# Gated mix of 32-head attention and a bilinear FFN on one core: a re-planned static schedule, x transposed on TensorE, one activation table, dead buffers reused as exponential tiles

## The chip, the core and the metric

The kernel runs on one core of a Trainium2 chip. The metric is the device time in microseconds (us) of one execution. The engines are TensorE (PE: matmuls; PEld: its weight loads), VectorE (DVE), ScalarE (ACT), GpSimd (POOL) and SyncE (SP, which here only issues DMAs). They run side by side, each works through its own instructions in order, and they wait for each other by semaphores.

## The reference, cut to what matters

```
x  [2048, 512] bf16, 32 heads of 16, F = 1376
g  = sigmoid((x * gate_w).sum(-1))
q, k, v = x @ wqkv
p  = softmax(q k^T / 4)            # per head, 2048 x 2048
a  = (p v) @ wo
b  = ((x @ w_gate) * (x @ w_up)) @ w_down
out = g * a + (1 - g) * b
```

## The kernel before, in words

**Work.** Queries come in 4 chunks of 512, heads in 4 blocks of 8, and a block's heads in two halves of 4. One chunk, block and half is a group: 32 groups, each of 4 heads x 16 key tiles = 64 score tiles of 128 keys x 512 queries, 2048 in all. A visit (L957) issues 2 to 4 score matmuls at once, one head in each 32-row strip of the array, into as many of the 8 PSUM banks. Each score tile is then turned into exponentials in a 512-column cell of the SBUF buffer `PT`, in one of two ways:

- ACT: one instruction for 1, 2 or 3 tiles (L1023), an exact exponential.
- DVE: an integer approximation (L1087) that writes the bits of a bf16. It needs three further copies with an added offset (L1039 on POOL, L1040 on DVE; `NP` = 4 variants in all), each multiplied with a V of its own scaling, so such a tile costs four PV matmuls instead of one.

PV matmuls (L1354; four heads in the four 32-column strips) accumulate a group into one bank, with a column of ones that gives the softmax denominator. Four matmuls that run side by side in the four strips are called a pack here.

**After each group** (`norm`, L1193 and following): DVE copies the bank to `oraw` (L1300); a DMA gathers the denominators into `den4`; DVE takes the reciprocal (L1222); a DMA writes it to `rscr` in DRAM. After the second half of a block four DMAs move rows of `oraw`, a DMA broadcasts `rscr` into `rb`, and POOL multiplies (L1278) into `OT`. All these DMAs go through SP's queue, between the weight loads.

**Products** (`_Fill`, tile4 at L454): K, Q, V, up, gate, down and output projection products of 4 or 11 packs each are put between scores and PV as "fills"; DVE evicts each.

**The order is a plan made when the program is built.** A loop simulates the engines with one cost per instruction: `a_cad(n)` for ACT, `d_cad`/`d_fast` for DVE, `p_cad` for POOL, a latency to the reader each (`A_LAT`, `D_LAT`, `P_LAT`), `PEC` for a pack, `PSW` for a change between row and column tiling, and for each DMA an issue cost (0.08 us) and a time to landing (2.0 to 2.4 us in `norm`, L1203 to L1268). At each simulated moment a policy per engine picks what is ready: `pe_policy` a visit, an urgent fill (`need` close), a PV pack, then any fill; `dve_policy` evictions, exponentials, copies; `pool_policy` first the OT products, then copies. The result is a fixed list of instructions per engine; on the chip each list runs in order whatever the real times are.

**Start and tail.** x of chunk 0 is loaded in 4 DMAs by SP, transposed by 16 TensorE matmuls of 128 columns (L487) and evicted by DVE (L506); chunks 1 to 3 are loaded by 12 transposing DMAs. All of w_down is loaded once into `wd`. The last group has its denominators in a bank of their own (L1365), and in the tail ACT takes Ln (L1557) and Exp (L1558) on four column slices; per slice DVE multiplies (L1561), PE multiplies with `wol` (L1566), DVE combines (L1575) and SP writes the output.

`PT` has `NC` = 34 cells; `xT`, `wk`, `wq`, `wv`, `wug`, `wd`, `hT` are buffers of their own.

Of the kernel before, what the change touches and what calls it, by code (L numbers as in the profile page):

```python
# [143 lines left out]
class _Fill:  # L144

    __slots__ = ("name", "packs", "deps", "evac", "need", "pos", "bank", "ok")

    def __init__(self, name, packs, deps, evac, need=10**9, ok=None):
# [25 lines left out]
def _build(nc, A_x, A_wqkv, A_wo, W_gate, W_up, W_down, gate_w, out):  # L174
# [22 lines left out]
    NC = 34  # L197
    NW = 4
# [7 lines left out]
    SLK = -0.1  # L206
# [4 lines left out]
    A_LAT = 0.24  # L211

    def d_cad(n):
        return 0.09 + n / 960.0

    def d_fast(n):
        return 0.09 + n / 3840.0

    D_LAT = 0.1

    def p_cad(n):
        return 0.2 + n / 1200.0
# [7 lines left out]
    with ExitStack() as stack:  # L230
# [4 lines left out]
        xT = sb("xT", [128, KD, S], BF16)  # L235
        wk = sb("wk", [128, KD, D], BF16)
        wq = sb("wq", [128, KD, D], BF16)
        wv = sb("wv", [128, KD, D], BF16)
        wo = sb("wo", [128, NB, D], BF16)
        wol = sb("wol", [128, D], BF16)  # L240
        wug = sb("wug", [128, NW, 2, KD, 128], BF16)
        wd = sb("wd", [128, FT, D], BF16)
# [4 lines left out]
        PT = sb("PT", [128, NC, 512], I16)  # L247
        OT = sb("OT", [128, 6, 512], BF16)
        hT = sb("hT", [128, FT, 512], BF16)
# [8 lines left out]
        idt = sb("idt", [128, 128], BF16)  # L258
        gex = sb("gex", [128, T], F32)
# [3 lines left out]
        warm = sb("warm", [128, 1], F32)  # L263
# [3 lines left out]
        free = {"pe": 0.3, "act": 0.3, "dve": 0.3, "pool": 0.3, "sp": 0.3}  # L267
# [75 lines left out]
        def dma(rank, dst, src, deps, stream, dur, after=None, eng="sp", **kw):  # L343
            def go(t):
                def fn(e):
                    return e.dma_start(dst, src, **kw)  # L346

                o = issue(eng, t, 0.08, dur, fn, deps(), stream, 16)
                if after is not None:
                    after(o)  # L350
                return o

            sq.append(_Job(rank, 0.08, deps, go))

        def now_dma(eng, dst, src, stream, dur, deps=(), **kw):
            t = max(free[eng], vis(deps))
            return issue(eng, t, 0.08, dur, lambda e: e.dma_start(dst, src, **kw), list(deps), stream, 16)
# [4 lines left out]
        xn = PT[:, 0:4, :].bitcast(BF16)  # L362
        wcol = lambda lo, hi: A_wqkv[:, lo:hi].rearrange("(kt p) n -> p kt n", p=128)
        d_xn = []
        for tt in range(4):
            d_xn.append(now_dma("sp", xn[:, tt, :], x2[tt * 128 : (tt + 1) * 128, :], f"dxn{tt}", 2.2))
        d_wk, d_wq = [None] * NB, [None] * NB
        d_wq[0] = now_dma("act", wq[:, :, 0:128], wcol(0, 128), "dwq0", 2.4)
        d_wk[0] = now_dma("act", wk[:, :, 0:128], wcol(D, D + 128), "dwk0", 2.6)
        d_wv = now_dma("act", wv[:, :, :], wcol(2 * D, 3 * D), "dwv", 4.0)  # L370
        d_xt = [None] * NCH
        for ch in range(1, NCH):
            for kt in range(KD):
                d_xt[ch] = now_dma(
                    "sp",
                    xT[:, kt, ch * 512 : (ch + 1) * 512],
                    x2[ch * 512 : (ch + 1) * 512, kt * 128 : (kt + 1) * 128],
                    f"dx{ch}",
                    2.0,
                    transpose=True,  # L380
                )
            d_xt[ch].vis = 6.0 + 5.0 * ch
            at(d_xt[ch].vis)
        free["sp"] = 4.0
        r_ = now_dma("act", wk[:, :, 128:D], wcol(D + 128, 2 * D), "dwk1", 6.0)
        d_wk[1:] = [r_] * (NB - 1)
        r_ = now_dma("act", wq[:, :, 128:D], wcol(128, D), "dwq1", 7.0)
        d_wq[1:] = [r_] * (NB - 1)
        d_gw = now_dma("act", gw[:, :], gate_w.rearrange("(kt p) -> p kt", p=128), "dgw", 7.0, allow_slow_non_contiguous=True)

        o_wz = now("dve", 0.1, 0.1, lambda v: v.memset(warm[:], 0.0))
        o_act = now("act", 1.4, 0.2, lambda a: a.activation(warm[:], warm[:], ACT.Exp), [o_wz])
        o_iz = now("dve", 0.1, 0.1, lambda v: v.memset(idt[:], 0.0))
# [5 lines left out]
                idt[:], idt[:], pattern=[[-1, 128]], compare_op=ALU.not_equal, fill=1.0, base=0, channel_multiplier=1  # L399
            ),  # L400
            [o_iz],
        )
        m0 = now("dve", 0.1, 0.1, lambda v: v.memset(mask[:], 0.0))
# [27 lines left out]
        def v_cols(k, t):  # L431
# [3 lines left out]
        ev_x = [None] * KD  # L435
        xdep = lambda ch: [ev_x[kt] for kt in range(KD)] if ch == 0 else [d_xt[ch]]
# [6 lines left out]
            "pvq": 0,  # L443
            "port": None,
# [39 lines left out]
        def mk_x(kt):  # L484
            def pk(tt):
                def f(pe, bank):
                    return pe.matmul(  # L487
                        ps[:, bank, tt * 128 : (tt + 1) * 128],
                        xn[:, tt, kt * 128 : (kt + 1) * 128],
                        idt[:],  # L490
                        start=True,
                        stop=True,
                        skip_group_check=True,
                    )

                return f

            def evac(bank, last):
                def after(o):
                    ev_x[kt] = o  # L500
                    release(banks[bank], [o])
                    if kt == KD - 1:
                        for c_ in range(4):
                            release(cells[c_], [o])

                dve_job(0, d_cad(512), lambda: [last], lambda v: v.tensor_copy(xT[:, kt, 0:512], ps[:, bank, :]), after)  # L506

            return _Fill("x", [pk(tt) for tt in range(4)], lambda: d_xn + [o_id], evac, 0)

        def mk_k(b, ch):  # L510
            def evac(bank, last):
                def after(o):
# [17 lines left out]
                    lambda kt: xT[:, kt, ch * 512 : (ch + 1) * 512],  # L530
# [3 lines left out]
                128 * b + 16 * ch,  # L534
            )

        def mk_q(b, c):
            s = (NB * c + b) % NQB

            def evac(bank, last):  # L540
                def after(o):
# [35 lines left out]
                    lambda kt: xT[:, kt, c * 512 : (c + 1) * 512],  # L577
# [4 lines left out]
                lambda: n < 0 or (n, 1) in q_last,  # L582
            )

        def mk_v(t):
            def evac(bank, last):
# [20 lines left out]
                prod(KD, 128, lambda kt, a, e: xT[:, kt, t * 128 + a : t * 128 + e], lambda kt: wv[:, kt, :]),  # L607
                lambda: [d_wv] + xdep(t // 4),
                evac,
                10**7,  # L610
# [4 lines left out]
        def mk_gate():  # L615
            def pk(q):
                def f(pe, bank):
                    r = None
                    for i in range(8 * q, 8 * q + 8):
# [3 lines left out]
                            xT[:, kt, t * 128 : (t + 1) * 128],  # L623
# [34 lines left out]
            return _Fill("gate", [pk(q) for q in range(8)], lambda: [d_gw] + xdep(0) + d_xt[1:], evac, 200)  # L658
# [4 lines left out]
        def load_w(c, f):  # L663
            n = c * FT + f
            w = FW[f]
            for i, src in enumerate((W_up, W_gate)):

                def after(o, i=i):
# [3 lines left out]
                    5 + n,  # L672
                    wug[:, n % NW, i, :, 0:w],
                    src[:, f * 128 : f * 128 + w].rearrange("(kt p) n -> p kt n", p=128),
                    lambda i=i: [w_free.get((n - NW, i))] if n >= NW else [],
                    f"dwug{n % NW}_{i}",
                    2.6,
                    after,
                )
                sq[-1].alt = (lambda i=i: n < NW or (n - NW, i) in w_free)  # L680

        def mk_ug(c, f, i):
# [18 lines left out]
            def evac_g(bank, last):  # L701
                w_free[n, 1] = last

                def after(o):
# [16 lines left out]
                    lambda kt, a, e: wug[:, n % NW, i, kt, a:e],  # L721
                    lambda kt: xT[:, kt, c * 512 : (c + 1) * 512],
# [6 lines left out]
                and (i == 0 or (n in ocopy and (c == 0 or (c - 1, 3) in d_end))),  # L729
            )  # L730
# [3 lines left out]
        def mk_d(c, tt):  # L734
# [14 lines left out]
            def evac(bank, last):  # L749
# [17 lines left out]
                lambda: [d_wd["d"]] + [ev_h[c, f] for f in range(FT)],  # L767
                evac,
                10**9,
                lambda: "d" in d_wd and all((c, f) in ev_h for f in range(FT)) and "g" in ogate and (c == 0 or (c - 1, tt) in bfree),  # L770
# [58 lines left out]
        fills += [mk_x(kt) for kt in range(KD)] + [mk_q(0, 0), mk_k(0, 0)]  # L829
        fills += [mk_v(t) for t in range(4)] + [mk_k(0, 1)] + [mk_v(t) for t in range(4, 8)] + [mk_k(0, 2)]  # L830
        fills += [mk_v(t) for t in range(8, 12)] + [mk_k(0, 3)] + [mk_v(t) for t in range(12, 16)]
# [12 lines left out]
        for c in range(NCH):  # L844
            for f in range(FT):
                load_w(c, f)
        dma(
# [8 lines left out]
        for j in range(4):  # L856
# [9 lines left out]
        dma(  # L866
            3,
            wd[:, 0 : FT - 1, :],
            W_down[0 : (FT - 1) * 128, :].rearrange("(f p) n -> p f n", p=128),
            lambda: [d_xt[NCH - 1]],  # L870
            "dwd",
            8.0,
        )
        dma(
            3,
            wd[0 : FW[-1], FT - 1, :],
            W_down[(FT - 1) * 128 : F, :],
            lambda: [d_xt[NCH - 1]],
            "dwd",
            8.0,  # L880
            lambda o: d_wd.__setitem__("d", o),
        )

# [21 lines left out]
        def visit(t, n, fb):  # L905
# [4 lines left out]
            if n >= 3 and load < DTH and ndve() < 3:  # L910
                nd = 1
                if n == 4 and load < 0.4 and acts > 0.6:
# [4 lines left out]
            for _ in range(nd):  # L917
                cand = [u for u in us if u not in ds]
                ok = []
                for u in cand:  # L920
# [6 lines left out]
                    if m == 0 and kt < 6:  # L927
# [220 lines left out]
        def dve_policy(t):  # L1148
# [16 lines left out]
            if best is not None and best.rank <= 1:  # L1165
                dq.remove(best)
                best.go(t)
                return True
            if dve_pass(t):
# [23 lines left out]
        def norm(m):  # L1193
# [8 lines left out]
            def after(o):  # L1202
                release(banks[bank], [o])  # L1203
                o_tail["o", m] = o
                row0 = 16 - p
# [6 lines left out]
                    2.0,  # L1212
                    dened,
                )
# [11 lines left out]
            def reced(o2):  # L1226
# [6 lines left out]
                    2.0,  # L1233
                    scred,
                )
# [381 lines left out]
```

## Time and profile before

| what | value |
| --- | --- |
| time, median of 3 runs (all) | 816.77 us (817.53, 809.5, 816.77) |
| the profiled execution | 821.65 us |
| its span, first to last instruction | 818.7 us |
| mean granted TensorE clock | 0.937 |
| busy PE / ACT / DVE / POOL | 741.0 / 734.4 / 634.1 / 472.1 us |
| L1023, exponentials on ACT | 720.0 us in 795 instructions |
| first exponential starts, last one ends | 16.75 us, 801.95 us |

A busy PE is not one at its peak, since the ends of pipelined matmuls are modelled: PE counts as busy for nine tenths of the span, though a pack follows the next in about 0.22 us when nothing holds it. In a line of waits the columns are who waited for whom, us in total, how often, and the longest. In a line of windows they are the window, its length, and busy us (instructions) of PE, PEld, DVE, ACT and POOL, then the granted TensorE clock (1.00 or 0.50 at any moment), the DMA share and GB/s.

### The profile page before, as it was taken

How to read it: one execution, taken by the hardware profiler on the slowest of the kernel's cores; microseconds unless marked ns; L12 is line 12 of the kernel's file. 1: busy time of each engine (PE TensorE's matmuls, PEld its weight loads, DVE VectorE, ACT ScalarE, POOL GpSimd, SP SyncE). 2: the span in 40 equal slices, each digit the busy share in tenths (PEclk: the TensorE clock that was granted, in tenths of full speed). 3: DMA queues.
4: the chain of work that ended last, by engine and by line, in shares of the span. 5: the costliest groups of instructions: out<-in, count | busy, mean ns of one | idle time of the engine just before them, and what ended most of it. 6: DMA issues, size and time to landing. Idle time of an engine off the chain costs nothing.

```text
span 818.7 us, 22335 instructions
## 1 busy us (share of the span) xinstructions
PE 741.0 (91%) x8917; PEld 214.3 (26%) x8917; DVE 634.1 (77%) x1232; ACT 734.4 (90%) x814; POOL 472.1 (58%) x538
## 2 busy tenths in 40 slices
PE   5999998998999989898989989899999998998993
PEld 2232322222322222222222222223222222222220
DVE  4798787786787888787885868858898887869682
ACT  2889897997999999899997979979999998989797
POOL 2456666535566665476654665625676676546460
PEclk9999997897999999999997979979999998999597
DMA  8600011121001111110021111100211100000000
GB/s 173 158 3 4 20 22 40 28 51 34 16 22 34 42 21 51 34 35 21 10 54 28 27 44 35 40 3 8 53 29 34 38 22 2 19 6 2 21 9 26
DMA packets 73478, 27.01 MB, mean 33 GB/s; under 512 B 64384, under 2 KB 70432, under 8 KB 73376
## 3 DMA queue, kind: packets, MB, share of 16 engines
q1 hardware_dynamic: 70208, 24.02, 12.9%
q10 hardware_dynamic: 3168, 1.57, 0.8%
q8 instruction: 71, 1.16, 0.6%
q14 instruction: 31, 0.25, 0.1%
HBM read 19.43 MB, written 2.35 MB: 27 GB/s over the span
## 4 chain that ended last, share of the span: by engine, by line
PE 38%; ACT 32%; DVE 8%; issue 7%; DMA 6%; POOL 4%; SPq 4%; ACTq 0%; DVEq 0%; POOLq 0%
ACT PT L1023 31%; PE ps L1354 13%; PE ps L454 13%; PE ps L957 12%; DMA rb<-rscr 5%; DVE PT L1087 5%; SPq L346 3%; POOL PT L1039 3%; DVE PT L1040 2%; POOL OT L1278 1%; DMA PT<-in_A_x_dram 1%; ACT L1558 1%; ACT L1557 1%; PE ps L1365 1%; DVE VV L603 0%
## 5 line engine op out<-in xcount | busy, mean ns | idle before, releaser
L1023 ACT ACTIVATE PT<-ps 128x1024 bf16<-128x1024 f32 (+2 forms) x795 | 720.0, 1029 | 74.3 <-PE ps L957 38.1
L1039 POOL TENSOR_SCALAR PT<-PT 128x1024 int16<-128x1024 int16 (+1 forms) x478 | 428.8, 918 | 242.6 <-DVE PT L1040 178.7
L1087 DVE TENSOR_SCALAR PT<-ps 128x512 int16<-128x512 f32 (+1 forms) x490 | 339.7, 708 | 97.3 <-PE ps L957 73.0
L1354 PE MATMUL ps<-PT,VV 128*32 128x512 bf16 x3581 | 317.2, 404 | 24.3 <-POOL PT L1039 13.4
L957 PE MATMUL ps<-QT,KT 32*128 32x512 bf16 (+1 forms) x2048 | 278.2, 399 | 28.4 <-ACT PT L1023 20.2
L1040 DVE TENSOR_SCALAR PT<-PT 128x512 int16<-128x512 int16 (+1 forms) x455 | 167.2, 421 | 2.2 <-PE ps L1354 0.5
L957 PEld LDWEIGHTS ps<-QT,KT 32*128 32x128 bf16 (+1 forms) x2048 | 70.5, 91 | 308.9 <-ACT PT L1023 98.0
L1354 PEld LDWEIGHTS ps<-PT,VV 128*32 128x32 bf16 x3581 | 81.8, 97 | 168.5 <-issue 83.8
L454 PE MATMUL ps<-xT,wug 128*32 128x512 bf16 x1376 | 123.1, 414 | 1.7 <-DVE PT L1087 0.9
L454 PE MATMUL ps<-wd,hT 128*32 128x512 bf16 (+1 forms) x704 | 53.2, 397 | 0.2 <-DVE PT L1087 0.2
L1278 POOL TENSOR_TENSOR OT<-oraw,rb 128x512 bf16<-128x512 f32 x16 | 20.5, 1281 | 45.9 <-DMA rb<-rscr 42.4
L697 DVE CAST usb<-ps 128x512 bf16<-128x512 f32 (+1 forms) x44 | 30.1, 684 | 18.0 <-PE ps L454 17.7
L454 PEld LDWEIGHTS ps<-xT,wug 128*32 128x32 bf16 x1376 | 30.5, 98 | 46.4 <-issue 32.6
L712 DVE TENSOR_TENSOR hT<-ps,usb 128x512 bf16<-128x512 f32 (+1 forms) x44 | 30.0, 682 | 8.3 <-PE ps L454 8.0
L454 PE MATMUL ps<-xT,wq 128*32 128x512 bf16 x256 | 21.1, 401 | 1.3 <-DVE xT L506 1.2
L1300 DVE COPY oraw<-ps 128x512 f32<-128x512 f32 x31 | 21.1, 680 | 0.2 <-PE ps L1354 0.2
L760 DVE TENSOR_SCALAR bsb<-ps,omg 128x512 bf16<-128x512 f32 x16 | 12.0, 748 | 11.7 <-PE ps L454 11.5
L593 POOL TENSOR_SCALAR VV<-VV 128x528 bf16<-128x528 bf16 x15 | 9.5, 633 | 19.7 <-DVE VV L593 15.2
L454 PE MATMUL ps<-wo,OT 128*32 128x512 bf16 x240 | 20.4, 407 | 0.0
L454 PE MATMUL ps<-xT,wk 128*32 128x512 bf16 x256 | 20.3, 397 | 0.0
L454 PEld LDWEIGHTS ps<-wd,hT 128*32 128x32 bf16 (+1 forms) x704 | 14.6, 97 | 21.6 <-issue 13.7
L546 POOL TENSOR_SCALAR QT<-QT,mask 128x512 bf16<-128x512 bf16 x16 | 11.1, 696 | 15.5 <-DVE QT L566 15.4
(51 smaller groups left out, 154.3 us busy)
## 6 DMA issues: line engine op xcount, KB each, us to landing
wug<-in_B_w_up_dram SPq DMA_DIRECT2D x40, 128.0 KB, 2.2
wug<-in_B_w_gate_dram SPq DMA_DIRECT2D x40, 128.0 KB, 2.2
rb<-rscr SPq DMA_DIRECT2D x15, 256.0 KB
out_dram<-ost SPq DMA_DIRECT2D x16, 128.0 KB, 1.7
oraw<-oraw SPq DMA_DIRECT2D x60, 32.0 KB, 2.0
wd<-in_B_w_down_dram SPq DMA_DIRECT2D x1, 1280.0 KB, 6.5
PT<-in_A_x_dram SPq DMA_DIRECT2D x4, 128.0 KB, 4.0
wv<-in_A_wqkv_dram ACTq DMA_DIRECT2D x1, 512.0 KB, 7.6
```

The source lines that it names most:

```text
L346: return e.dma_start(dst, src, **kw)
L454: r = pe.matmul(ps[32 * i : min(w, 32 * i + 32), bank, :], lhs(32 * i, min(w, 32 * i + 32)), rhs, start=s0, stop=s1, tile_position=(0, 32 ...
L697: lambda v: v.tensor_copy(usb[0:w, n % 2, :], ps[0:w, bank, :]),
L712: lambda v: v.tensor_tensor(hT[0:w, f, :], ps[0:w, bank, :], usb[0:w, n % 2, :], ALU.mult),
L957: r = pe.matmul(ps[:, bank_of[u], :], KT[32 * j : e, b, kt * 128 : (kt + 1) * 128], QT[32 * j : e, s, p, :], start=True, stop=True, tile_p ...
L1023: lambda a: a.activation(span(PT, cs).bitcast(BF16), span(ps, bs), ACT.Exp, scale=ESC),
L1039: return lambda e: e.tensor_scalar(span(PT, ds), span(PT, cs), 1.0, float(SH[k]), ALU.mult, ALU.add)
L1040: return lambda e: e.tensor_single_scalar(span(PT, ds), span(PT, cs), float(SH[k]), ALU.add)
L1087: lambda v: v.tensor_scalar(span(PT, cs), span(ps, bs), IOFF, 0.0, ALU.add, ALU.max),
L1278: lambda g: g.tensor_tensor(OT[:, pair % 6, :], oraw[:, 0, :], rb[:, :], ALU.mult),
L1300: lambda v: v.tensor_copy(oraw[:, p, :], ps[:, bank, :]),
L1354: r = pe.matmul(ps[32 * j : 32 * j + 32, ob, :], v_ap(k, kt, 8 * b + 2 * j + p, p), PT[:, cell, :].bitcast(BF16), start=f0, stop=stops[m, ...
```

## The change

It has nine parts:

1. The plan's costs: ACT's latency 0.24 to 0.17, DVE 0.09 + n/960 to 0.068 + n/960 with latency 0.1 to 0.12, POOL 0.2 to 0.157 + n/1200; a DMA issue 0.08 to 0.4-0.66 us, the broadcast into `rb` 2.4 to 3.7 us; the four moves of `oraw` are issued before the reciprocals are written and no longer after.
2. x of all chunks is loaded untransposed and transposed on TensorE in packs of four 32-column matmuls; chunk 0 is loaded in two DMAs from two queues, and two of its four evictions go to ACT. Only two loads are left on ACT's queue.
3. 24 matmuls on a zero tile at the start.
4. One table with Ln and Exp is loaded at the start, instead of Exp there and an Ln and an Exp load in each slice of the tail.
5. `xT`, `wk`, `wq`, `wv`, `hT`, `wd` and the up/gate weights lie in `PT`. 42 cells are exponential tiles from the start (eight of them once they have held x), and those of each buffer are added when its last reader is done (92 in the end).
6. w_down is loaded anew in each chunk, in five pieces of two tiles and one of 96 rows, into the place of the up/gate weights (now 5 pairs of slots).
7. PACE: fills are urgent while their packs are behind 1.03 times the share of score tiles done; a started fill goes on before new urgent ones and PV; one free bank is enough to start one.
8. No DVE exponential for the first 16 key tiles of group 0 (before: 6); two DVE exponentials from one visit allowed up to a DVE load of 0.8 us (before: 0.4).
9. `SLK` -0.1 to 0.0: a visit of fewer than four tiles may be put 0.1 us later.

The diff, cut to its core:

```diff
-    NC = 34
-    NW = 4
+    NA = 42
+    NC = NA + 8 + 16 + 4 + 2 * 11
+    NW = 5
...
-    SLK = -0.1
+    VN = 1000
+    D0 = 16
+    BURST = 1
+    FB = 1
+    D2 = 0.8
+    EV = 0
+    SLK = 0.0
+    PACE = 1.03
...
-    A_LAT = 0.24
+    A_LAT = 0.17
...
-        return 0.09 + n / 960.0
+        return 0.068 + n / 960.0
...
-        return 0.2 + n / 1200.0
+        return 0.157 + n / 1200.0
...
+        wk = PT[:, c_k : c_k + KD, :].bitcast(BF16)
...
+        hT = PT[:, c_h : c_h + FT, :].bitcast(BF16)
+        wd = PT[:, c_w : c_w + FT, :].bitcast(BF16)
...
-        d_xt = [None] * NCH
+        d_xn = [[xload("sp", 0, 0, 2, "dxa", 2.6), xload("act", 0, 2, 4, "dxb", 2.6)]]
+        d_wk[0] = now_dma("sp", wk[:, :, 0:128], wcol(D, D + 128), "dwk0", 3.0)
+        d_wq[0] = now_dma("act", wq[:, :, 0:128], wcol(0, 128), "dwq0", 3.0)
+        now("act", 1.35, 0.2, lambda a: a.preload_act_table_set("natural_log_exp_and_others"))
+        d_wv = now_dma("sp", wv[:, :, :], wcol(2 * D, 3 * D), "dwv", 4.5)
         for ch in range(1, NCH):
-            for kt in range(KD):
-                d_xt[ch] = now_dma(
...
-                    transpose=True,
...
+            d_xn.append([xload("sp", ch, 0, 4, f"dx{ch}", 4.0 + ch)])
...
+        for _ in range(24):
+            now(
+                "pe",
+                0.11,
+                0.3,
+                lambda pe: pe.matmul(ps[:, 7, 0:128], idz[:], idz[:], start=True, stop=True, skip_group_check=True),
+                [o_iz],
+            )
...
-                    dma(0, rb[:, :], bc, lambda: w + [prev, o_rbz], "drb", 2.4, lambda o: rbed(o, mv))
+                    dma(0, rb[:, :], bc, lambda: w + [prev, o_rbz], "drb", 3.7, lambda o: rbed(o, mv), 0.66)
...
+        def done_with(key, o):
+            r = refs[key]
+            r[0] -= 1
+            if r[0] == 0:
+                for x in r[1]:
+                    release(cells[x], [o])
...
+            late = st["packs"] < PACE * st["u"] * n_packs / NU
...
-                    if urgent_only and f.need > pos + 40:
+                    if urgent_only and f.need > pos + 40 and not late:
...
+            if BURST and st["fill"] is not None and fill_pack(t, False):
+                return True
             if fill_pack(t, True):
                 return True
```

In the built programs the lists change as follows (instructions; a "tile" is one score tile):

| | before | after |
| --- | --- | --- |
| score tiles on ACT (instructions of 3, 2, 1 tiles) | 1537 (87, 568, 140) | 1515 (84, 562, 139) |
| score tiles on DVE | 511 | 533 |
| offset copies on POOL (2 tiles, 1 tile) | 331, 147 | 396, 103 |
| offset copies on DVE (2 tiles, 1 tile) | 269, 186 | 279, 146 |
| PV matmuls in strips | 3581 + 112 | 3647 + 112 |
| x transposes | 16 of 128 columns | 256 in strips |
| evictions of x | 4 DVE | 14 DVE, 2 ACT |
| activation table loads | 9 | 1 |
| score tiles between the last up/gate/down fill and the closing fills | 115 (1856 to 1970) | 207 (1778 to 1984) |

More of the change, by code (lines that the diff above doesn't have):

```diff
@@ L443, in _build @@
             "pvq": 0,
+            "packs": 0,
             "port": None,
@@ L499, in after @@
                 def after(o):
-                    ev_x[kt] = o
+                    ev_x[ch, kt] = o
                     release(banks[bank], [o])
[L502 to L508, printed above, removed]
+                    done_with(("xn", ch), last)
+                if ch == 0 and kt % 2:
+                    aq_small.append(
+                        (0.48, [last], lambda a: a.activation(xT(kt, 0, 512), ps[:, bank, :], ACT.Identity), after)
+                    )
+                    return
+                dve_job(
+                    0,
+                    d_cad(512),
+                    lambda: [last],
+                    lambda v: v.tensor_copy(xT(kt, ch * 512, (ch + 1) * 512), ps[:, bank, :]),
+                    after,
+                )
+            return _Fill("x", [pk(tt) for tt in range(4)], lambda: d_xn[ch] + [o_id], evac, 0)
         def mk_k(b, ch):
@@ L846, in _build @@
                 load_w(c, f)
+            load_d(c)
         dma(
@@ L911, in visit @@
                 nd = 1
-                if n == 4 and load < 0.4 and acts > 0.6:
+                if n == 4 and load < D2 and acts > 0.6:
                     nd = 2
@@ L1168, in dve_policy @@
                 return True
+            if EV and best is not None:
+                dq.remove(best)
+                best.go(t)
+                return True
             if dve_pass(t):
@@ L1241, in scred @@
                     w = [o_tail["rec", m - i] for i in range(p + 1)]
-                    oo = [o_tail["o", m - i] for i in range(p + 1)]
                     if single:
@@ L1429, in fill_pack @@
                     return False
-                if not urgent_only and fu.need > 10**8 and len(fb) < 2:
+                if not urgent_only and not late and fu.need > 10**8 and len(fb) < FB:
                     return False
@@ L1509, in _build @@
         policies = [("dve", dve_policy), ("act", act_policy), ("pool", pool_policy), ("pe", pe_policy), ("sp", sp_policy)]
-        for c_ in range(4):
-            cells[c_].at = INF
-        for kt in range(KD):
-            pass
         at(0.3)
```

266 lines of the change are left out of this document (158 added, 108 removed).

## Prediction, written before the changed kernel ran

> **What bounds the kernel now.** I read the page's busy line first, then the groups by shape, the waits of ACT, and windows of the trace.
>
> ```profile
> PE 741.0 (91%) x8917; PEld 214.3 (26%) x8917; DVE 634.1 (77%) x1232; ACT 734.4 (90%) x814; POOL 472.1 (58%) x538
> ```
>
> PE's 91% is not a bound: 8829 strip matmuls are 2207 packs, and packs follow each other 0.22 us apart where nothing holds them, 486 us in all. ACT is the bound. Windows of everything between the first and the last exponential, then of the tail, show it:
>
> ```profile
> 16.75:801.95 785.20, 730.13 (x8829) 210.03 (x8821) 624.20 (x1210) 720.26 (x796) 468.72 (x525) 0.94 0.13 30
> 801.95:818.72 16.77, 3.80 (x16) 0.84 (x16) 4.87 (x9) 12.61 (x16) 0.00 (x0) 0.65 0.09 31
> ```
>
> So the span is 16.75 us of lead-in, 785.2 us with ACT busy for 720.3 (65.0 idle), and 16.8 us of tail. The waits of ACT tell what the idle time waits for: late score tiles (L957; 11.0 of the 38.1 us are the start) and cells of `PT` not yet free, released by PV or by copies (17.4 + 11.2 + 4.2 = 32.8 us).
>
> ```profile
> ACT PT L1023 <- PE ps L957: 38.1, 43, 11.0
> ACT PT L1023 <- PE ps L1354: 17.4, 24, 2.3
> ACT PT L1023 <- POOL PT L1039: 11.2, 8, 2.4
> ...
> ACT PT L1023 <- DVE PT L1040: 4.2, 4, 1.9
> ```
>
> Then the clock, which runs at 1.00 or 0.50. One case at 132 us, from SP's, POOL's and PE's timelines and a window:
>
> ```profile
> 128.27 0.66 SPq L346 DMA_DIRECT2D rb<-rscr  x1
> ```
>
> ```profile
> 132.48 1.26 POOL L1278 TENSOR_TENSOR OT<-oraw,rb 128x512 bf16<-128x512 f32 x1 [2.70 <-DMA rb<-rscr]
> 133.71 3.25 POOL L1039 TENSOR_SCALAR PT<-PT 128x512 int16<-128x512 int16 x4
> ```
>
> ```profile
> 134.38 0.56 PE L1354 MATMUL ps<-PT,VV 128*32 128x512 bf16 x4 [1.89 <-POOL PT L1039]
> ```
>
> ```profile
> 134.50:148.10 13.60, 13.60 (x101) 2.58 (x97) 7.13 (x16) 8.80 (x9) 5.57 (x6) 0.50 0.10 20
> ```
>
> The broadcast takes 4.21 us from its issue to L1278, where the plan has 0.08 + 2.4. POOL stands 2.70 us in front of L1278, the copies queued behind it are late, PV waits 1.89 us for them, and for the next 13.6 us PE runs at half rate: ACT is idle for 4.8 of them. This repeats:
>
> ```profile
> POOL OT L1278 <- DMA rb<-rscr: 42.4, 15, 4.9
> ```
>
> Nine stretches inside the run are at half rate, 92.2 us in sum with ACT busy for 64.58, so 27.6 us idle (30%). The nine at full rate after 90 us are 623.1 us with 593.47 busy: 29.6 idle (4.8%). L1278 stood waiting 2.0 to 6.7 us before seven of the nine half-rate stretches began (134.5, 189.1, 335.9, 428.0, 482.6, 530.4, 677.2). Every gap in PE's timeline of 1.2 us or more from 20 us to the last exponential (longest 2.28) comes at one of these seven.
>
> **The change part by part.** The sum is made on the profiled execution: 821.65 us, that is its span 818.7 and 2.95 around it. It lies 4.9 above the median of 816.77, probably by its half-rate stretches; I aim at absolute time.
>
> *Lead-in, -4.5.* x lands at 8.29 us now, after four issues and in the traffic of other loads. The x row of the DMA list has a median of 4.0 us to landing; from an issue that ends at 1.2 this gives 5.3 (-3.0; if the halves land as late as today, 0). Transposes and evictions take 8.53 to 11.69 = 3.2 us, four evictions on DVE at 0.62 in a row; two on each engine give about 2.4 (-0.75). Q and K then take eight packs at 0.42 us, half rate; the 24 zero matmuls, which run while PE waits for x, may lift this to 0.22 (0 to -1.7, I take -0.75). Ends -0.7 and -5.5. ACT's 0.2 us warm-up goes; its one load (1.28 us) lies ahead of x either way.
>
> *Chunks 1 to 3 of x, 0.* 48 more packs of 128 columns: between a quarter of 0.22 and the 0.12 us of today's x matmuls, 2.6 to 5.8 us of PE, which has 300 to spare; 12 DVE evictions of 0.62 = 7.4 us. In 16.75 to 86.7 us ACT is idle for 69.95 - 62.26 = 7.7 us; evictions added may double that, the missing DVE exponentials of group 0 and the missing transposing DMAs (19.4 us of SP's queue) may empty it: -7.7 to +7.7, I take the middle.
>
> *Fewer tiles on ACT, -10.2.* By shape, 3, 2 and 1 tiles cost 126.6/87 = 1.455, 550.6/568 = 0.969, 83.2/140 = 0.594. Before that sums to 760.4 against 720.0 without overlap, after to 749.6, so 709.8. The 22 tiles go to DVE: exponentials +11.7, copies -6.9, x +6.2, V copies -2.3, total about 643 us. POOL: 396 x 1.031 + 103 x 0.605 = 471 of copies against 430, with V copies about 517. Both have room in 770; if not, the gain is 0 (rival B).
>
> *Tail, -6.6.* The loads of 8 x 1.283 us go.
>
> ```profile
> 801.95 1.28 ACT L1557 ACT_TABLE_LOAD   x1
> 803.25 0.28 ACT L1557 ACTIVATE oraw<-ps 128x128 f32<-128x128 f32 x1
> 803.54 1.28 ACT L1558 ACT_TABLE_LOAD   x1
> 804.84 0.31 ACT L1558 ACTIVATE rb<-oraw 128x128 f32<-128x128 f32 x1
> ```
>
> What they covered appears: the last PV (ends 0.65 after the last exponential), then 0.65 for Ln and Exp, then DVE in order: multiply 0.29, PE 0.39 to 0.61, combine 0.75 and gaps, 1.57 to 1.79 per slice, four in series, then 2.15 for the last output. That is 9.7 to 10.6 in place of 16.8.
>
> *DMA times and clock, -12.6.* The plan now has 0.66 + 3.7 = 4.36 us for the broadcast against 4.21, and 0.6 for each move on SP (2.49 measured for four). L1278's wait should fall from 42.4 to between 0 and 7 us. The seven stretches are 68.3 us with 22.4 idle; at 4.8% it would be 3.3: -19.1. I give back 4 for one that stays (the costliest has 5.45 idle), and 2.4 for the end: score tiles without any product are now 207 in a row, not 115, and the half-rate stretch inside them at 755.7 has 3.93 idle of 20.5, 2.9 too many; 80% more of it.
>
> *More cells, -15.* 42 for 34, 50 when `wk` and `wv` are used up, 92 at last. Of the 32.8 us for cells about half (29.6 of 57.2) is at full rate, 17; I take 15. Ends 0 (copies free cells as late as before) and -17.
>
> *No price.* 22 more w_down DMAs are some 11 us of a queue that mostly waits; their tiles hang on the last up/gate matmul and the next chunk's weights on the last down product, so at three chunk ends no FFN product can start for some 5 us (two landings of 2.2 us or more). Scores and PV cover that; without the cover PE has a gap (rival C). PACE, `BURST`, `FB`, `D2` and `SLK` move products and visits by fractions of a us; their price is in the chances.
>
> Sum: -4.5 - 10.2 - 6.6 - 12.6 - 15 = -48.9, so 772.8. Cross-check: 12.25 + 709.8 + idle 37.4 + 10.2 + 2.95 = 772.6.
>
> **The rivals.** *A, more: nothing at half rate.* All 27.6 us fall to 4.8% of 92.2: -23.2 where I have -12.6, so 762; with the whole 17 for cells 760, and lower with fewer full-rate stalls. For it: every long PE gap belongs to L1278. Against: the stretch at 755.7 began without a gap over 0.7 us, in windows with few packs, and that part grows. The Trainium skill, page "TensorE: Matmul & The Clock Gate", Part 1, says that the clock halves after an idle window of about 3.4 us; this kernel would then never slow down inside, which is A. The trace agrees on the length (stretches of 3.4 to 20.5 us) and not on the cause: gaps of 1.2 to 2.3 us were enough, so I give A no more for it.
>
> *B, less: POOL and the copies become the bound.* POOL and DVE copies keep out of each other's way:
>
> ```profile
> POOL PT L1039 <- DVE PT L1040: 178.7, 134, 8.9
> ```
>
> Together they are 517 + 166 = 683 us of some 745 (92%) where they are 472 + 172 of 785 (82%). From 29 to 798 us POOL idles 297; if all but the 42.4 stays, 517 + 255 = 772 and the exponentials last as long as today: 821.65 - 4.5 - 6.6 = 810. Halfway is 791. Against: the new costs match the rows (two-tile copy 1.010 planned, 1.031 measured), so the plan knows of it.
>
> *C, slower: PE gaps move and the clock stays down.* One us at half rate costs ACT 0.30 - 0.05 = 0.25 us. With no product PE took 19.6 us for 64 tiles at full rate (729.9 to 749.5) and 27.0 mostly at half (749.5 to 776.5). If the 207 tiles all ran at half (87 us) and each of 15 block ends, in a plan with less slack, still brought 10 us, it would be 240 us at half: 773 - 6 + 60 = 827. From 200 us on it is no gain, from 233 on over 1% slower. Against: the gaps seen have one cause, and the plan now has its time.
>
> That the change does not do what it says is excluded for loads, tiles and cells by the instruction lists; for the wait it is B or C.
>
> **How the numbers follow.** Forecast (760 to 790): 0.55. A, under 760: 0.17. B, 790 to 811: 0.18, of which 0.03 within 1%. C: 0.10, of which 0.08 over 1% slower. A measurement here tells 1% from no change (808.6 to 825). Faster 0.55 + 0.17 + 0.15 = 0.87, same 0.05, slower 0.08. The range 752 to 806 leaves out the lower part of A (0.07), C, and the top of B (0.03).
>
> **What would show it.** Right: L1278's wait under 10 us, at most 45 us at half rate and these late, ACT busy near 710 before the tail, first exponential at 11 to 14 us, tail near 10 us, ACT's waits for PV and copies under 15. Wrong: POOL over 90% busy with ACT waiting for copies (B); over 150 us at half rate (C); PE gaps at the chunk ends; L1278 still waiting 2 us or more.

## Result, and the profile after

| | before | after |
| --- | --- | --- |
| time, median of the runs | 816.77 us | 744.73 us (744.37, 744.73, 752.99) |
| ratio to before on the same chip, with its 95% interval | 1 | 0.9175 [0.9049, 0.93] |
| profiled execution, span | 821.65, 818.7 | 744.73, 742.7 |
| lead-in, to the first exponential | 16.75 | 11.77 |
| first to last exponential | 785.2 | 720.2 |
| ACT busy in it, idle in it | 720.3, 65.0 | 705.0, 15.3 |
| at half clock, ACT idle in that | 92.2, 27.6 | 47.8, 9.3 |
| at full clock, ACT idle in that | 693.0, 37.3 | 672.4, 6.0 |
| tail | 16.79 | 10.71 |

Faster by 8%, and by 28 us more than forecast: the time lies below the range. An execution more than 1.5% above the fastest of its kernel counts as slow, and the ratios and medians leave it out. The page's busy line of the kernel after:

```profile
PE 716.6 (96%) x9246; PEld 212.6 (29%) x9247; DVE 637.8 (86%) x1201; ACT 709.4 (96%) x797; POOL 513.5 (69%) x566
```

ACT is busy for 96% of the span where it was 90%. There is little but ACT's own work left, so ACT's waits are short. In order: who waited for whom, us in total, times, longest.

```profile
ACT PT L1119 <- PE ps L1053: 13.3, 16, 4.8
ACT PT L1119 <- PE ps L1455: 3.5, 7, 1.5
...
ACT PT L1119 <- DVE PT L1183: 0.2, 1, 0.2
```

L1119 is the exponential, L1053 the score matmul, L1455 the PV matmul (before: L1023, L957, L1354). Of the 13.3 us for scores 4.8 are the start. The waits for a free cell, 32.8 us before in three lines, are 3.5 us, and no wait for a copy on POOL is listed. The waits of POOL, for the multiply into `OT` (now L1379):

```profile
POOL OT L1379 <- DVE PT L1136: 13.4, 6, 5.6
```

Its wait for the broadcast, 42.4 us before, is gone; it waits only for DVE. Windows of the kernel after, cut where the granted clock changes (columns as before: busy us of five engines, then the clock):

```profile
11.77:78.40 66.63, 64.14 (x982) 21.37 (x975) 54.85 (x109) 64.36 (x73) 37.76 (x53) 1.00 0.18 42
78.40:85.20 6.80, 6.59 (x80) 2.87 (x80) 5.85 (x11) 4.47 (x6) 5.77 (x7) 0.50 0.11 41
85.20:648.40 563.20, 553.01 (x7233) 161.45 (x7229) 504.91 (x937) 560.76 (x626) 415.49 (x439) 1.00 0.17 42
648.40:665.40 17.00, 16.64 (x122) 3.21 (x122) 11.39 (x21) 14.82 (x18) 12.31 (x13) 0.50 0.04 15
665.40:685.90 20.50, 16.81 (x189) 4.95 (x185) 19.48 (x42) 20.30 (x23) 10.94 (x15) 1.00 0.01 2
685.90:709.80 23.90, 23.70 (x180) 4.64 (x176) 17.07 (x33) 19.14 (x18) 15.56 (x18) 0.50 0.07 18
```

Read the third line: for 563.2 us on end, three quarters of the run, ACT is idle for 563.20 - 560.76 = 2.44 us, 0.4%. Before, the full-rate stretches after 90 us had 4.8%. Half rate is left in three places only: at 78.4, and twice late, in the stretch of score tiles without products. In sum 9.3 us of idle time lie there.

Lead-in and tail, from the timelines of PE and ACT (start, duration, engine, line, what, count):

```profile
4.48 1.90 PE L519 MATMUL ps<-idt,PT 128*32 128x128 bf16 x64 [0.75 <-DMA PT<-in_A_x_dram]
7.12 4.21 PE L484 MATMUL ps<-PT 128*32 128x512 bf16 x48 [0.74 <-DVE PT L547]
```

```profile
733.65 0.28 ACT L1660 ACTIVATE oraw<-ps 128x128 f32<-128x128 f32 x1 [1.65 <-PE ps L1466]
733.96 0.31 ACT L1661 ACTIVATE rb<-oraw 128x128 f32<-128x128 f32 x1
734.18 0.26 ACT L1660 ACTIVATE oraw<-ps 128x128 f32<-128x128 f32 x1
```

The first transpose of x starts at 4.48 us instead of 8.53. The products of Q, K and V that come next are 12 packs in 4.21 us: the first seven follow each other 0.42 us apart, then, at 10.1 us, the trace's record of the granted clock begins, at 1.00, and the rest come 0.22 us apart. So seven of the eight packs of Q and K still run at the slow pace. In the tail Ln and Exp follow each other with no load between them.

### The profile page after: what moved, and what is told of

It is laid out like the page before. It is cut to its first block, busy times and chain, and to the rows that moved or that the text cites. A ratio compares the mean times of both kernels' runs of the same rounds, so it can differ in the third digit from the quotient of the medians.

```text
span 742.7 us, 22849 instructions
## 1 busy us (share of the span) xinstructions
PE 716.6 (96%) x9246; PEld 212.6 (29%) x9247; DVE 637.8 (86%) x1201; ACT 709.4 (96%) x797; POOL 513.5 (69%) x566
## 4 chain that ended last, share of the span: by engine, by line
PE 67%; ACT 22%; DVE 6%; issue 4%; DMA 1%; ACTq 0%; DVEq 0%
PE ps L1455 24%; ACT PT L1119 22%; PE ps L1053 22%; PE ps L484 20%; DVE PT L1183 2%; DVE PT L1136 2%; PE ps L1466 1%; DMA PT<-in_A_x_dram 0%; DMA den<-oraw 0%; DVE ost L1678 0%; PE ps L1669 0%; PE ps L519 0%; DVE VV L648 0%; PE ps L667 0%; DVE PT L794 0%
## 5 line engine op out<-in xcount | busy, mean ns | idle before, releaser
L1119 ACT ACTIVATE PT<-ps 128x1024 bf16<-128x1024 f32 (+2 forms) x785 | 704.7, 1027 | 18.5 <-PE ps L1053 13.3
L1135 POOL TENSOR_SCALAR PT<-PT 128x1024 int16<-128x1024 int16 (+1 forms) x499 | 465.9, 958 | 166.3 <-DVE PT L1136 140.8
L1455 PE MATMUL ps<-PT,VV 128*32 128x512 bf16 x3647 | 301.6, 398 | 5.8 <-ACT PT L1119 3.4
L1053 PE MATMUL ps<-QT,KT 32*128 32x512 bf16 (+1 forms) x2048 | 273.0, 395 | 8.8 <-ACT PT L1119 3.5
L484 PE MATMUL ps<-PT 128*32 128x512 bf16 (+1 forms) x2848 | 225.5, 386 | 3.6 <-DVE PT L547 0.9
L1136 DVE TENSOR_SCALAR PT<-PT 128x1024 int16<-128x1024 int16 (+1 forms) x425 | 157.3, 428 | 0.9
L1053 PEld LDWEIGHTS ps<-QT,KT 32*128 32x128 bf16 (+1 forms) x2048 | 68.6, 91 | 281.3 <-ACT PT L1119 81.7
L1455 PEld LDWEIGHTS ps<-PT,VV 128*32 128x32 bf16 x3647 | 77.5, 96 | 133.1 <-issue 74.0
L484 PEld LDWEIGHTS ps<-PT 128*32 128x32 bf16 (+1 forms) x2848 | 59.2, 95 | 91.7 <-issue 55.2
L794 DVE TENSOR_TENSOR PT<-ps,usb 128x512 bf16<-128x512 f32 (+1 forms) x44 | 29.9, 680 | 5.0 <-PE ps L484 4.9
L638 POOL TENSOR_SCALAR VV<-VV 128x528 bf16<-128x528 bf16 x24 | 15.3, 637 | 23.6 <-DVE VV L638 20.9
L1379 POOL TENSOR_TENSOR OT<-oraw,rb 128x512 bf16<-128x512 f32 x16 | 20.4, 1273 | 14.4 <-DVE PT L1136 13.4
L648 DVE CAST VV<-ps 128x512 bf16<-128x512 f32 x16 | 10.9, 688 | 8.3 <-PE ps L484 8.2
L610 DVE TENSOR_SCALAR QT<-ps 128x512 bf16<-128x512 f32 x16 | 10.9, 681 | 3.7 <-PE ps L484 3.7
L563 DVE CAST KT<-ps 128x512 bf16<-128x512 f32 x16 | 10.9, 680 | 2.6 <-PE ps L484 2.4
```

Of the source, the lines that this page charges most:

```text
L484: r = pe.matmul(ps[32 * i : min(w, 32 * i + 32), bank, :], lhs(32 * i, min(w, 32 * i + 32)), rhs, start=s0, stop=s1, tile_position=(0, 32 ...
L638: return lambda e: e.tensor_scalar(v_cols(k, t), v_cols(0, t), CW[k], 0.0, ALU.mult, ALU.add)
L794: lambda v: v.tensor_tensor(hT[0:w, f, :], ps[0:w, bank, :], usb[0:w, n % 2, :], ALU.mult),
L1053: r = pe.matmul(ps[:, bank_of[u], :], KT[32 * j : e, b, kt * 128 : (kt + 1) * 128], QT[32 * j : e, s, p, :], start=True, stop=True, tile_p ...
L1119: lambda a: a.activation(span(PT, cs).bitcast(BF16), span(ps, bs), ACT.Exp, scale=ESC),
L1135: return lambda e: e.tensor_scalar(span(PT, ds), span(PT, cs), 1.0, float(SH[k]), ALU.mult, ALU.add)
```

## The experiments

The question: where do 28 us more than forecast come from? Idle time of ACT fell by 65.0 - 15.3 = 49.7 us, where 27.6 were forecast (12.6 for DMA times, 15 for cells). One theory: the two causes are separate and each is worth far more than its term, so that they add. The rival: one of them brings nearly all, and the other only backs it up. Further questions were the engine costs, the stretch without products, the half rate at 78 us, the table, and the zero matmuls. No experiment leaves out any of the computation. All ratios are to the kernel before, on the same chip; after's own is 0.9175. What is said in us against after is across chips, on which the medians of the kernel before lie up to 8.5 us apart.

**1. After, with the old DMA times in the plan.** The order of the moves of `oraw`, early, stays.

```diff
-        def dma(rank, dst, src, deps, stream, dur, after=None, cost=0.4, **kw):
+        def dma(rank, dst, src, deps, stream, dur, after=None, cost=0.08, **kw):
...
-                    dma(0, rb[:, :], bc, lambda: w + [prev, o_rbz], "drb", 3.7, lambda o: rbed(o, mv), 0.66)
+                    dma(0, rb[:, :], bc, lambda: w + [prev, o_rbz], "drb", 2.4, lambda o: rbed(o, mv), 0.08)
```

> The changed kernel, planned with the old DMA times again (issue 0.08 us each, broadcast 2.4 us; the moves stay early). Theory 1, the measured DMA times removed the stalls and with them most idle time of ACT at both clock rates: the product of oraw and rb waits about 30 to 45 us for the broadcast again, half rate on 90 us or more, time 770 to 785 us. Theory 2, the extra cells removed them, and late DMAs are then absorbed: waits for the broadcast return, but half rate stays under 70 us and the time is 745 to 760.

0.9568 [0.9483, 0.9654]; 779.77 us, 35 more than after, as theory 1 has it. The waits of POOL, then of ACT:

```profile
POOL OT L1379 <- DMA rb<-rscr: 22.0, 10, 4.0
```

```profile
ACT PT L1119 <- PE ps L1053: 31.0, 45, 4.6
ACT PT L1119 <- PE ps L1455: 6.5, 9, 1.5
ACT PT L1119 <- POOL PT L1135: 4.8, 7, 1.6
```

The broadcast is waited for again (22.0 us, less than the 30 to 45 that theory 1 expected), half rate goes from 47.8 to 95.6 us, and what ACT waits for is late scores, 31.0 for 13.3 us. Idle time rises at half rate (26.2) and at full rate too (17.6 for 6.0).

**2. After, with 34 cells throughout and none handed on.**

```diff
-    NA = 42
+    NA = 34
...
-            if r[0] == 0:
+            if r[0] == 0 and key[0] == "xn":
```

> The changed kernel with 34 exponential cells from start to end, used-up buffers not handed on. Theory 1 (DMA times): under 755 us, since late DMAs, not too few cells, made ACT wait. Theory 2 (cells): ACT waits 15 us or more for PV and copies to free cells, time 760 to 775 us.

0.9543 [0.9441, 0.9645]; 775.72 us, 31 more than after, at the upper end of theory 2. The waits of ACT:

```profile
ACT PT L1119 <- PE ps L1455: 26.4, 33, 2.4
ACT PT L1119 <- PE ps L1053: 14.1, 20, 3.8
```

Here the scores are on time (14.1 for 13.3) and the cells are not: 26.4 us for PV to free one, 3.5 in after. No wait for the broadcast came back. The two edits make two different waits.

**3. Both at once**: the edits of 1 and 2 together.

> The changed kernel with both undone: the old DMA times in the plan and 34 cells from start to end. Alone each cost about 34 us. Theory 5 (two causes that add): 808 to 818 us. Theory 8, they partly stand in for each other (a late broadcast makes copies late, which a larger stock of cells bridges): less than the sum, 785 to 805 us.

1.0115 [1.0062, 1.0169]; 819.54 us, 74.8 more than after; the two alone gave 35.0 and 31.0, 66.0 in sum. So they add, and neither stands in for the other; the 9 us beyond the sum are about what executions of one of these kernels differ by. The waits of ACT show both:

```profile
ACT PT L1119 <- PE ps L1455: 34.2, 40, 4.1
ACT PT L1119 <- PE ps L1053: 33.3, 41, 4.3
```

With both undone the kernel is even slower than before by 1%, although lead-in (11.22) and tail (9.56) keep their gain. Laid out as a square, ACT's idle time from first to last exponential, each corner from one profiled execution:

| idle us: half rate + full rate | old DMA times | new DMA times |
| --- | --- | --- |
| 34 cells | 36.3 + 40.8 (3) | 14.7 + 29.6 (2) |
| all cells | 26.2 + 17.6 (1) | 9.3 + 6.0 (after) |

Read along the rows: DMA times take 17 to 22 us at half rate, and 11 to 12 at full rate. Down the columns: cells take 23 to 24 at full rate, and 5 to 10 at half rate. Each is worth 28.5 to 33.3 us of idle time in all. The rest of the 74.8 us is mostly ACT's busy time: 720.4 in 3, 711.7 in 1, 713.5 in 2, 705.0 in after.

The corner with both undone is not the kernel before, which idles for 65.0 us: it keeps the other parts of the change, and with them it idles for 77.0, 12 us more.

**4. Cells fixed at 42**, none handed on (only the second of the two edits of experiment 2).

> The changed kernel with 42 cells from start to end: no used-up buffer is handed on. If the first 8 extra cells are what matters, 744 to 753 us and ACT's waits for PV stay under 10 us. If the cells handed on during the run matter as much, 758 to 770 us.

0.953 [0.9449, 0.9611]; 773.72 us, more than expected: 8 cells beyond 34 bring 2 us, which is not clear of the noise, and the handing on of used-up buffers 29. ACT waits 14.4 us for PV and 22.5 for scores. It idles for 23.3 us at half rate and 14.2 at full, where after has 9.3 and 6.0: the cells handed on act at both rates.

**5. Before, with only the new DMA times** (issue costs, landing times and the broadcast's 3.7 + 0.66; the order of the moves stays).

```diff
-        def dma(rank, dst, src, deps, stream, dur, after=None, eng="sp", **kw):
+        def dma(rank, dst, src, deps, stream, dur, after=None, cost=0.4, eng="sp", **kw):
...
-                    dma(0, rb[:, :], bc, lambda: w + [prev, o_rbz], "drb", 2.4, lambda o: rbed(o, mv))
+                    dma(0, rb[:, :], bc, lambda: w + [prev, o_rbz], "drb", 3.7, lambda o: rbed(o, mv), 0.66)
```

> The kernel before, planned with the changed kernel's times for the DMAs of the normalisation (issue 0.4 to 0.66 us, broadcast 3.7 us) and nothing else. Theory 5, DMA times and cells are two causes that add: the wait for the broadcast falls under 8 us, half rate under 45 us, but ACT still idles 25 us or more at full rate for want of cells; 782 to 797 us. Theory 6, with 34 cells PE gets its gaps from cells anyway: half rate stays over 60 us, 798 to 812 us.

0.9615 [0.9546, 0.9685]; 777.86 us. So about half of the whole change's gain comes from a few numbers in the plan. Theory 5 holds, with a time somewhat below its range. Half rate falls from 92.2 to 34.1 us, and no PE gap over 0.72 us is left. ACT's idle time from first to last exponential falls from 65.0 to 32.1 us: 27.6 to 8.4 at half rate, and 37.3 to 23.7 at full rate. From the waits of ACT:

```profile
ACT PT L1023 <- PE ps L957: 19.1, 16, 10.8
ACT PT L1023 <- PE ps L1357: 15.0, 23, 1.9
```

Without the start's 10.8 us late scores cost 8.3 us, where they cost 27.1; what stays is mainly cells (L1357 is PV here), as in experiment 2. But the waits for cells shrink too: with 4.6 us for copies they are 19.6 us, where they were 32.8, though the number of cells is the same.

**6. Before, with only the new engine costs.**

```diff
-    A_LAT = 0.24
+    A_LAT = 0.17
...
-        return 0.09 + n / 960.0
+        return 0.068 + n / 960.0
...
-        return 0.2 + n / 1200.0
+        return 0.157 + n / 1200.0
```

> The kernel before, planned with the changed kernel's engine costs and latencies alone. 29 fewer tiles on ACT are 13 us. Theory 3 (exact costs matter by themselves): 790 to 803 us. Rival, the stalls at the broadcast decide and a tighter plan only meets more of them: 803 to 822 us with over 80 us at half rate.

1.0414 [1.0369, 1.0458], 844.31 us: slower, outside of both expectations. ACT's exponentials do get fewer (1508 tiles for 1537), and the waits eat it up. ACT, then POOL:

```profile
ACT PT L1023 <- PE ps L957: 40.9, 41, 11.2
ACT PT L1023 <- PE ps L1354: 39.4, 37, 4.5
ACT PT L1023 <- POOL PT L1039: 14.7, 10, 3.5
```

```profile
POOL OT L1278 <- DMA rb<-rscr: 39.0, 15, 3.9
```

The late broadcasts still cost 39.0 us on POOL, and ACT's wait for PV goes from 17.4 to 39.4 us. A reading that fits, but that no run tests by itself: the old engine costs were too long, and so held the slack that the too short DMA times lacked; without it the copies behind a late broadcast have no room.

**7. After, with the old engine costs** (the reverse of that diff).

> The changed kernel planned with the old engine costs and latencies (ACT latency 0.24; DVE 0.09 + n/960; POOL 0.2 + n/1200). 16 more tiles on ACT are 7 us. Theories 1 and 2: 750 to 758 us, no more than those tiles and small gaps. Theory 3, the exact engine costs let the plan fill the gaps at full rate: 765 to 780 us with ACT idle over 4% at full rate.

0.9326 [0.925, 0.9402]; 758.12 us, 13 more than after. ACT has 1531 tiles for 1515 and is busy 9 us longer; its idle time at full rate stays at 5.9, and at half rate it is 14.6 for 9.3. So theory 3 fell. The same three costs gain 13 us in the kernel after and lose 4% in the kernel before. The DMA times are not the only difference between the two: with right DMA times and 34 cells, before with the old engine costs (experiment 5) idles for 32.1 us, and after with the new ones (experiment 2) for 44.4. So the cells may matter as much for this as the DMA times; no run separates them.

**8. Products to the end: two free banks needed to start one.**

```diff
-    FB = 1
+    FB = 2
```

> The changed kernel, but a product that is not urgent needs two free banks to start, as before. In the instruction list products then reach to the last score tile, and the 207 tiles without any are gone. Theory 4, half rate after 640 us comes from the missing products: these 41 us of half rate vanish, ACT idles 6 us less there, 735 to 742 us. Rival: it comes from the PV matmuls of four cells or the last loads, or two banks cost stalls elsewhere: half rate of 30 us or more remains, 744 to 755 us.

0.922 [0.909, 0.9351], not to be told from after. In the profiled execution only 10.2 us are at half rate. What that gives (ACT idle 12.0 for 15.3) goes back in the tail, 15.2 us for 10.7, into which products of `wo` fall. This is the fastest of four executions, 744.42 us at a mean granted clock of 0.992; the others took 754.68 to 760.88 us at 0.963 to 0.975, which at rates of 1.00 and 0.50 is 38 to 56 us at half rate, the tail included. So the rival's 30 us or more at half rate show in three of four, though products reach to the end.

**9. The same from tile 1200 on only.**

```diff
-                if not urgent_only and not late and fu.need > 10**8 and len(fb) < FB:
+                if not urgent_only and fu.need > 10**8 and len(fb) < (FB if st["u"] < 1200 else 2):
```

> The changed kernel, but from score tile 1200 on a product that is not urgent needs two free banks: products reach to tile 1988 and the first part of the plan is unchanged. Theory 4 (missing products bring half rate): under 20 us of half rate after 600 us, 736 to 743 us. Rival: half rate comes back with small PE gaps, in some executions only: 743 to 755 us with a spread of 8 us or more.

0.9195 [0.9144, 0.9246]: no difference either (741.5 to 748.57 us). The late half rate is gone from the profiled execution, and two other stretches, at 467.5 and 597.2, stand in its place. In the later one 40 matmuls of products run, and PE has no gap over 0.43 us in the 10 us before it. So missing products are not the only thing that brings half rate.

**10. The gate later.** At 78.4 us the clock halves though PE has no gap over 0.3 us. What runs there are the gate's matmuls, 64 of one column each, among scores. PE's timeline in after:

```profile
77.69 0.39 PE L1053 MATMUL ps<-QT,KT 16*128 16x512 bf16 x3 [0.21 <-ACT PT L1119]
78.01 0.35 PE L667 MATMUL ps<-gw,PT 128*128 128x1 bf16 x8
78.60 0.61 PE L1053 MATMUL ps<-QT,KT 16*128 16x512 bf16 x3 [0.24 <-ACT PT L1119]
```

The score triple takes 0.39 us at 77.69 and 0.61 at 78.60. The experiment puts the gate behind six up and gate products.

```diff
-                200,
+                10**9,
...
-        fills += [mk_gate()]
...
+                if f == 5 and c == 0:
+                    fills += [mk_gate()]
```

> The changed kernel with the gate's 64 one-column matmuls put after the first six up and gate products of chunk 0. Theory 7, these matmuls bring the half-rate stretch at 78 to 85 us, although PE has no gap there: that stretch goes, and one appears within 7 us of the gate's new place; 742 to 750 us. Rival, it comes from the first block's end: it stays at 75 to 90 us.

The gate then runs from 147.9 to 153.3 us, and windows of that kernel read:

```profile
78.00:85.00 7.00, 6.96 (x94) 2.04 (x90) 6.22 (x10) 7.00 (x8) 7.00 (x10) 1.00 0.15 41
147.50:150.70 3.20, 2.58 (x48) 1.42 (x46) 2.79 (x6) 3.20 (x4) 1.84 (x2) 1.00 0.00 0
150.70:157.50 6.80, 6.36 (x76) 2.17 (x72) 4.10 (x9) 6.01 (x7) 3.65 (x5) 0.50 0.01 2
```

The half rate has moved with the gate: its matmuls are the cause. The time does not change by more than can be told: 0.9215 [0.9132, 0.9298].

**11. Exp's own table at the start**, as before the change, so that the tail loads eight tables again.

```diff
-        now("act", 1.35, 0.2, lambda a: a.preload_act_table_set("natural_log_exp_and_others"))
+        o_gx0 = now("dve", 0.1, 0.1, lambda v: v.memset(gex[:], 0.0))
+        now("act", 1.4, 0.2, lambda a: a.activation(gex[:], gex[:], ACT.Exp), [o_gx0])
```

> The changed kernel with Exp alone loaded at the start, so that Ln and Exp are loaded again in each slice of the tail. By the prediction's working the tail grows from 10.7 us to 16 to 17.5, and nothing else moves: 750 to 752 us. Rival, the loads lay beside DVE's and PE's work: the tail stays under 13 us.

One run, 748.43 us; its tail takes 17.10 us for 10.71, so the one table is worth 6.4 us of tail (6.6 forecast). The time grows by only 3.7 us, since the lead-in was 9.85 us in this execution. The loads in the tail are 1.28 us each, as before:

```profile
732.93 1.28 ACT L1661 ACT_TABLE_LOAD   x1
734.22 0.28 ACT L1661 ACTIVATE oraw<-ps 128x128 f32<-128x128 f32 x1
734.51 1.28 ACT L1662 ACT_TABLE_LOAD   x1
```

**12. No zero matmuls at the start.**

```diff
-        for _ in range(24):
+        for _ in range(0):
```

> The changed kernel without the 24 zero matmuls. The first exponential starts at 12.5 to 14 us, since the products of Q and K all run at half rate (0.42 us a pack); with the zero matmuls it came at 9.7 to 11.9 us. Rival, the matmuls do nothing: 9.7 to 11.9 us again. The rest as the changed kernel, 744 to 754 us.

One run, 744.19 us, lead-in 11.67: as after, and below the 12.5 to 14 expected. In both the first six or seven packs are slow, until the record of the granted clock begins, at 1.00, at 9.8 us here and at 10.1 in after. In experiments 10 and 11, which have the zero matmuls, it begins at 3.9 and 4.3 us, and all packs are fast (the 48 matmuls in 2.77 us, lead-ins of 9.68 and 9.85). So zero matmuls do not bring the early full rate each time, and one run does not show whether they bring it at all. The Trainium skill, page "TensorE: Matmul & The Clock Gate", Part 1, says that the clock is judged over windows that run freely and do not start with the kernel, so that the point of the rise changes from run to run; that fits these four, and none of them tests it.

## Why the prediction was right on the direction and wrong on the size

The forecast was 12.25 lead-in + 709.8 busy + 37.4 idle + 10.2 tail + 2.95 around = 772.6. Measured: 11.77 + 705.0 + 15.3 + 10.71 + 2.03 = 744.8. The differences are -0.5, -4.8, -22.1, +0.5 and -0.9: four fifths lie in the idle time.

**Lead-in, right.** The transposes began about 1 us earlier than forecast (4.48, where x was put at 5.3); seven of the eight packs of Q and K stayed at the slow pace, from which 0.75 us had been hoped.

**Fewer tiles on ACT, right, a little too small.** 720.3 to 705.0 is -15.3 where -10.2 was put. The instructions' summed durations fell by 11.6 us (818.1 to 806.5), near what was worked out. The other 3.7 are overlap: fewer of them wait, so 731 begin before the one ahead has ended, where 686 did, by 0.14 us each.

**Tail, right.** -6.1 against -6.6, and experiment 11 gives 6.4 for the table alone.

**DMA times and clock, -12.6: the step that failed.** The mechanism was right: L1278's wait went from 42.4 to 0, and half rate from 92.2 to 47.8 us, with the late part of it left where the text put it. The size was not. Experiment 5 makes this one change on the kernel before, and ACT's idle time falls by 32.9 us. Of these 19.2 are at half rate, where the text put 19.1 for the seven stretches and gave 6.4 back. The other 13.6 are at full rate, where it counted nothing: a late broadcast also makes scores late while the clock is full. Of 27.1 us of late scores beside the start 8.5 remain in after. The square puts the DMA times at 28.5 to 32.8 us, 11 to 12 of them at full rate.

**More cells, -15: failed in the same way.** The text took the 32.8 us of waits for cells, called half of them full-rate, and set 0 and -17 as ends. The waits did go (to 3.5 us), but not by the cells alone: the DMA times take them to 19.6 (experiment 5). The square puts the cells at 29.0 to 33.3 us of idle time, of which 23 to 24 at full rate and the rest at half rate, which the text had left to the other term. So -17 was no bound.

Both terms came from one idle time, divided along the clock, and each cause reaches across that line. Idle time at full rate fell by 31.3 us, from 37.3 to 6.0, where the sum took off only the 15 for cells.

**A cost that was put at nothing.** In the square the two causes give 61.8 us, and the idle time fell by 49.7. The other 12 are what the kernel with both undone idles more than the kernel before: the other parts of the change cost them, and the sum had no such term. Which part does it is not shown; experiment 6, where the engine costs alone raise the idle time from 65.0 to 95.6 us, points at these. That the total missed by 28 us and not by 40 is luck.

**Rival A** had the better size, but not for its reason: "nothing at half rate" did not happen (47.8 us are left), and its 760 still had the full-rate waits in it. **Rival B** fell: POOL is busy for 69%, and ACT does not wait for its copies. **Rival C** fell for after, with 47.8 us at half rate against the 200 it needs; experiment 3, with 122.9 us, shows how the plan looks without the two gains.

**No price.** `PACE` and `BURST` were said to move products by fractions of a us. With `PACE` = 0 or `BURST` = 0 the built instruction lists are the same as after's; of the three only `FB` acts, and it gives the late stretch without products. `D2` and `SLK` were not tried. The chunk ends, where no FFN product can start, cost next to nothing: the longest PE gap there is 0.85 us, at 231.

**Open.** What starts the late half-rate stretches in after and those in mid run in experiments 8 and 9, and what makes the Q and K packs fast in some executions. Before with both the engine costs and the DMA times was not run: the planner finds no order for it.

## What to carry to other kernels

In a static schedule, put the measured times of the transfers into the plan first: DMA times that had a broadcast at 2.5 us, where it takes 4.2, cost 4% of the time in the kernel before and 35 us in the kernel after. Exact engine costs alone made the kernel before 4% slower, perhaps since they took away the slack that hid this error. When idle time is split between causes, do not split it by where it is seen; undo each cause alone and both together, and the square of four runs says if they add. Look for buffers that are dead before the end: handing them on as spare tiles was worth 29 us, eight fixed tiles more only 2.

## What the runs showed of the hardware that was not expected

The clock halves without an idle PE. 64 matmuls of one column, spread over 5 us among scores, bring 6.8 us at half rate in both places where they were put (experiment 10), with no PE gap over 0.3 us in after. At 648.4 and 685.9 us in after the clock halves among score tiles without products; that their absence is the cause is not shown (experiments 8 and 9). The same part of that page of the Trainium skill, "TensorE: Matmul & The Clock Gate", says that the half rate comes after an idle window of about 3.4 us; the trace agrees on the length of a window (6.8, 17.0 and 23.9 us are 2, 5 and 7 times 3.41, within 0.1) and not on the cause, since PE was seen busy for most of it.

Half rate does not cost ACT the same everywhere: 9.3 of 47.8 us (19%) in after against 27.6 of 92.2 (30%) before. It would fit that ACT has more to do while PE is slow when cells are spare, but experiment 9, with the same cells as after, has 10.4 of 34.1 us (31%). Within after it is 34% in the stretch at 78.4 us and 13 to 20% in the two late ones.
